# Two transformer layers on one core: 288 pairs of row maxima beside the projections in place of 223, and twelve pairs per eight key tiles in attention

## The chip, the core and the metric

The kernel runs on one core of a Trainium2 chip. The metric is device time in microseconds for one execution of the whole program, median of the runs. Inputs and outputs are float32 and lie in HBM.

## The reference

Two layers, each an attention block and a block with a squared ReLU, each with a layer norm ahead and a residual sum. The same weights serve both layers. There are 2048 rows of width 640, 32 heads of width 20, and a hidden width of 1536.

```python
def _A_ref(x, wqkv, wo):
    qkv = (x @ wqkv).reshape(B, S, 3, H, Dh)         # -> q, k, v per head
    scores = einsum("bhqd,bhkd->bhqk", q, k) * Dh ** -0.5
    o = einsum("bhqk,bhkd->bhqd", softmax(scores), v)
    return o.reshape(B, S, D) @ wo
def _B_ref(x, w1, b1, w2, b2):
    r = maximum(x @ w1 + b1, 0)
    return (r * r) @ w2 + b2

x = x + _A_ref(_layernorm(x), wqkv, wo)
x = x + _B_ref(_layernorm(x), w1, b1, w2, b2)
# ... and both once more
```

The softmax needs the largest score of each row before it exponentiates. What the change moves is the search for these maxima.

## The kernel before, in words

**Stages.** Each layer runs the projections (`qkv`), attention (`attention`), the output projection (`add_heads`) and the squared-ReLU block (`mlp`), one after the other. Between them q, k and v pass through HBM (`d_qk`, `d_v`).

**Blocks and tiles.** Heads are taken in eight groups of four (g = 0 to 7), queries in four blocks of 512 (qb). A block of attention is t = 4 g + qb, 32 in all. Keys are loaded in four quarters of 512 (c), one tile per group and quarter (`load_k`, L396), queries in one tile per block (`load_q`, L409), each with six DMAs on SP's queue. The key tiles are kept in three sets: group g takes the set g % 3, so the fourth group (g = 3) takes the memory of the first. Within attention a block goes over 16 key tiles of 128 keys (kt); this makes 512 key tiles in a layer.

**Two passes over the scores.** The kernel makes the scores twice. In the first pass the queries are rows, and VectorE takes each row's maximum over a quarter of the keys (the *maxima*). A unit of this work is a *pair*: two heads at once, 128 queries against one quarter of the keys, two matmuls (`by_queries`, L433). There are 8 pairs per block and quarter, 1024 in a layer. In the second pass, in attention, the keys are rows: one matmul per head and key tile (`score`, L499), with the negative maxima in two further rows of the query tile, then ScalarE's exponential (L506), then the products with v (`pv`, L511). The maxima of a block must all be there before its second pass: `mrows_max` (L462) joins the quarters, `mrows` (L474) transposes them on TensorE, and eight DMAs write them into the query tile.

**Where the maxima are made.** Some of the pairs run beside the projections: there TensorE makes two matmuls into two neighbouring banks, and VectorE reduces both with one instruction of 128x1024 (`smax_two`, L454). The others run inside attention, one bank and one instruction of 128x512 for each head (`smax`, L445), in a ring of three banks.

**Order beside the projections.** `qkv` emits 40 units of 15 matmuls (`proj_unit`, L304) and 16 units of 30 smaller ones for v (`v_unit`, L332). After each matmul it calls `between`, which adds 1 (0.65 in `v_unit`) to a counter; at 11 it emits three pairs in a burst (`some`). What it takes them from is `groups`, a list of (g, qb, c), each of eight pairs; when it begins one, it loads the tiles of that and of the next (`tiles`). The list is filled from `EARLY` as blocks of rows are projected: the first group of heads, and at the end of the first 16 units all sixteen entries of the second. At the end of the projections what is left of the list is dropped, and its pairs go to attention. Here this comes to 223 pairs per layer.

**Order in attention.** The engines' order is written out by strings in `ORDERS`: a and b are scores of even and odd heads, m and n the same for maxima, V the products of one key tile. One string covers eight key tiles (a *group of eight tiles* in what follows) with a given number of pairs, 12 to 16. `pairs()` chooses the string: it computes how many pairs per eight tiles are needed so that every block's maxima are made in time, and takes at least twelve. Over the 61 strings that have maxima left to make, before the change this is thirteen nearly everywhere and fourteen in five; the last strings make none. The string of twelve is there, but not used:

```python
13: "baanmbVmbanambbnbmVanbmnaVnaabnmbVanbmaanVnmbbanaVmnbmabVabbmmnaVm",
12: "naambbmVanmbambVbmannabVnabnmabVabnmbanVbbmnanaVbmmbaanVbmbmnaaV",
```

`op` emits one letter. For m and n it takes the next pair from `todo`; it emits nothing while that pair's keys or queries have not been asked for (`if (t // NQB, c) not in k_t or t not in q_t: return`). Keys are asked for in `begin(i)`, at the first score of key tile i: with block 4 (the first of g = 1, key tiles 64 to 79) come the four quarters of g = 3, at key tiles 65, 69, 73 and 77.

**Queues.** All these loads and stores are issued by SP in the order of the program. At the end of a block `finish` (L519) copies the sums out of the bank on ScalarE and stores four rows of them (`d_s`); these stores wait for the last product of the block, and what SP issues next stands behind them.

Of the kernel before, what the change touches and what calls it, by code (L numbers as in the profile page):

```python
# [25 lines left out]
NQB = S // QB  # L26
# [12 lines left out]
def tile_layers(  # L39
# [343 lines left out]
    k_t, q_t, v_t, mx_t, kept = {}, {}, {}, {}, {}  # L383
# [210 lines left out]
        [(0, qb, c) for qb in range(NQB) for c in range(NQB) if max(qb, c) == tb]  # L594
        for tb in range(NQB)
    ]
    EARLY[-1] += [(1, qb, c) for qb in range(NQB) for c in range(NQB)]

    FIRST = 4
    UNITS = [(tb, pos) for tb in range(NQB) for pos in range(FIRST)]
    UNITS += [(tb, pos) for pos in range(FIRST, 10) for tb in range(NQB)]

    def qkv(first, x_src, rest):
# [4 lines left out]
        state = {"pace": 0, "n": 0}  # L610
# [13 lines left out]
            else:  # L624
                at(early, n, lambda pos=pos: w_qk.need(pos * 10, pos * 10 + 9))
        for k in range(KD if first else w_v.n):
            n = len(UNITS) - 7 + k
            if first:
                at(early, n - 2, lambda k=k: raws.append(raw_rows(wqkv[:, 2 * D :], k)))
                at(late, n, lambda k=k: w_v.put(  # L630
                    raws.pop(0), k * 4, k * 4 + 2, 2, nc.scalar.copy, pool_lo
                ))
            else:
                at(early, n, lambda k=k: w_v.load(k))
# [18 lines left out]
        def end_group(x):  # L653
            g, qb, c = x
            t = g * NQB + qb
            left[t] -= 1
            if left[t]:
                return
            if t < 1:
                mrows_max(t)  # L660
                work.append(lambda: mrows(ps_q, t))
            elif t > 2:
                del q_t[t]
# [20 lines left out]

        def between(cost):
            state["pace"] += cost
            if state["pace"] >= 11:
                state["pace"] -= 11
                some()
            state["n"] += 1  # L690
            if state["n"] % 4 == 0:
                next(rest, None)

        for n, (tb, pos) in enumerate(UNITS):
            while tb not in xt_:
                next(rest)
            run(early, n)
            later(proj_unit(pos, tb, lambda: between(1)))
            run(late, n)
            if pos == FIRST - 2:  # L700
                tiles(EARLY[tb][0])
            if pos == FIRST - 1:
                groups.extend(EARLY[tb])
            if first:
                w_qk.save_full(1)
                w_v.save_full(1)
            if pos >= FIRST and tb == NQB - 1 or n == 4 * FIRST - 1:
                w_qk.past(pos * 10 + 9, w_qk.got)
# [370 lines left out]
```

## Time and profile before

| What | Value |
|---|---|
| Median of three runs | 3805.72 us (3802.45 to 3811.96) |
| The profiled execution | 3801.84 us, span 3799.8 us |
| TensorE's granted clock | 0.997 |
| Busy over the span | PE 3754.3, VectorE 2923.8, ScalarE 2399.9, GpSimd 813.0 us |
| Layer 1: first product of attention to the end of the last | 337.38 to 1487.87 us |
| Layer 2: the same | 2227.55 to 3376.36 us |
| Maxima beside the projections (L454), both layers | 446 instructions, 1220 ns each |
| Maxima in attention (L445), both layers | 3204 instructions, 685 ns each |

In the profile PE is TensorE's matmuls and PEld its weight loads; DVE is VectorE, ACT ScalarE, POOL GpSimd, and SPq SP's queue of DMA issues. Lines of a timeline begin with the start and the length in us and end in brackets with the idle time of the engine before and what ended it. Instructions of a kind that follow each other closely are one line, with their count behind the x. Matmuls are pipelined and their ends are modelled, so where TensorE's pace matters, the distance between starts is read and not the busy time. L511 has eight records per key tile.

### The profile page before, as it was taken

The page shows a single profiled execution, that of the slowest core. Times are in us where ns is not written, and L with a number is a line of the kernel's source. Part 1 is how long each engine was busy: PE and PEld are TensorE (multiplying, and loading weights), DVE is VectorE, ACT ScalarE, POOL GpSimd, SP SyncE. Part 2 cuts the span into 40 slices and gives each one's busy share as a digit, 9 for nine tenths or more (in the row PEclk, how much of TensorE's full clock was granted, in tenths as well). Part 3 has the DMA queues.
Part 4 walks back from the last instruction along what each step waited for, and adds up shares of the span by engine and source line. Part 5 has one row for each costly group of instructions (what it writes and reads, how often), then busy time and mean ns, then how long its engine had stood idle before and what let it go on. Part 6 is the DMA issues. An engine that isn't in the chain of part 4 may idle for free.

```text
span 3799.8 us, 62979 instructions
## 1 busy us (share of the span) xinstructions
PE 3754.3 (99%) x23636; PEld 2142.9 (56%) x23636; DVE 2923.8 (77%) x4436; ACT 2399.9 (63%) x4663; POOL 813.0 (21%) x889
## 2 busy tenths in 40 slices
PE   7999999999999999999999999999999999999999
PEld 5676444443443435988876754444444444369998
DVE  7999999999999992444469989999999999924443
ACT  2115999999999996122211159999999999951221
POOL 5430343221121111111143201211211111101110
PEclk9999999999999999999999999999999999999999
DMA  6553454322121135611244422222222211355111
GB/s 191 176 189 110 132 142 149 107 71 73 49 70 42 31 96 176 239 42 42 93 142 157 161 89 59 65 74 53 65 81 53 59 40 42 101 191 209 42 42 42
DMA packets 228073, 378.72 MB, mean 100 GB/s; under 512 B 47740, under 2 KB 96636, under 8 KB 227768
## 3 DMA queue, kind: packets, MB, share of 16 engines
q1 hardware_dynamic: 227224, 372.98, 31.1%
q8 instruction: 187, 3.06, 0.3%
q10 hardware_dynamic: 544, 1.71, 0.2%
q14 instruction: 118, 0.97, 0.1%
HBM read 243.00 MB, written 130.52 MB: 98 GB/s over the span
## 4 chain that ended last, share of the span: by engine, by line
PE 94%; DVE 3%; DMA 1%; ACT 1%; SPq 0%; issue 0%; POOL 0%; ACTq 0%; DVEq 0%; POOLq 0%
PE banks L511 26%; PE banks L293 20%; PE banks L499 18%; PE banks L433 18%; PE banks L304 6%; PE banks L332 4%; DVE mx L445 1%; DVE mx L454 1%; SPq L75 0%; PE banks L909 0%; PE banks L474 0%; ACT e L506 0%; DMA k<-d_qk 0%; DVE bst L252 0%; DVE h L265 0%
## 5 line engine op out<-in xcount | busy, mean ns | idle before, releaser
L506 ACT ACTIVATE e<-banks 128x512 f32<-128x512 f32 x4096 | 2113.8, 619 | 159.4 <-PE banks L499 104.7
L445 DVE TENSOR_REDUCE mx<-banks 128x1 f32<-128x512 f32 x3204 | 2002.5, 685 | 209.4 <-PE banks L433 147.5
L433 PE MATMUL banks<-k,q 60*128 60x512 f32 x4096 | 1197.5, 442 | 8.7 <-DMA q<-d_qk 4.1
L499 PE MATMUL banks<-q,k 62*128 62x512 f32 x4096 | 1174.9, 430 | 4.5 <-ACT e L506 1.7
L511 PE MATMUL banks<-e,vg 128*32 128x512 f32 x8192 | 1092.8, 605 | 0.0
L433 PEld LDWEIGHTS banks<-k,q 60*128 60x128 f32 x4096 | 580.7, 184 | 626.9 <-DVE mx L445 495.3
L499 PEld LDWEIGHTS banks<-q,k 62*128 62x128 f32 x4096 | 613.6, 185 | 438.6 <-ACT e L506 399.9
L454 DVE TENSOR_REDUCE mx<-banks 128x2 f32<-128x1024 f32 x446 | 518.8, 1220 | 49.6 <-PE banks L433 37.0
L555 POOL TENSOR_TENSOR few<-few,minus_t 128x16 f32<-128x16 f32 x62 | 179.8, 2901 | 991.1 <-DMA few<-d_s 975.3
L511 PEld LDWEIGHTS banks<-e,vg 128*32 128x32 f32 x8192 | 161.5, 108 | 346.0 <-issue 322.8
L293 PE MATMUL banks<-w,h 128*128 128x320 f32 x2304 | 352.8, 312 | 2.9 <-DVE h L265 2.7
L293 PEld LDWEIGHTS banks<-w,h 128*128 128x128 f32 x2304 | 340.9, 189 | 12.5 <-DVE h L265 6.8
L293 PE MATMUL banks<-xnT,w 128*128 128x512 f32 x1440 | 330.3, 390 | 0.0
L304 PE MATMUL banks<-xnT,wqk 128*128 128x512 f32 x1200 | 311.9, 407 | 0.0
L932 ACT ACTIVATE r<-banks,b_t 128x512 f32<-128x512 f32 x96 | 66.2, 690 | 375.2 <-PE banks L293 375.2
L293 PEld LDWEIGHTS banks<-xnT,w 128*128 128x128 f32 x1440 | 269.4, 188 | 55.3
L270 ACT COPY r<-banks 128x512 f32<-128x512 f32 x92 | 53.7, 588 | 334.9 <-PE banks L304 292.5
L304 PEld LDWEIGHTS banks<-xnT,wqk 128*128 128x128 f32 x1200 | 220.8, 192 | 68.9 <-issue 23.8
L952 DVE TENSOR_TENSOR x<-banks,x 128x320 f32<-128x320 f32 x128 | 62.8, 491 | 200.9 <-PE banks L293 194.9
L566 POOL TENSOR_TENSOR o<-o 128x512 f32<-128x512 f32 x62 | 79.5, 1282 | 560.0 <-PE banks L433 177.4
L933 DVE TENSOR_TENSOR r<-r 128x512 f32<-128x512 f32 x96 | 79.4, 827 | 132.6 <-ACT r L932 132.2
L887 DVE TENSOR_TENSOR x<-banks,x 128x320 f32<-128x320 f32 x64 | 31.0, 484 | 171.0 <-PE banks L293 77.7
(63 smaller groups left out, 1704.1 us busy)
## 6 DMA issues: line engine op xcount, KB each, us to landing
q<-d_qk SPq DMA_DIRECT2D x636, 80.0 KB
d_qk<-ev SPq DMA_DIRECT2D x80, 512.0 KB
k<-d_qk SPq DMA_DIRECT2D x384, 80.0 KB
x<-d_x SPq DMA_DIRECT2D x96, 320.0 KB
d_o<-ot SPq DMA_DIRECT2D x248, 80.0 KB
ot<-d_o SPq DMA_DIRECT2D x38, 512.0 KB
d_v<-v SPq DMA_DIRECT2D x32, 512.0 KB
vg<-d_v SPq DMA_DIRECT2D x32, 512.0 KB
```

The source lines that it names most:

```text
L293: nc.tensor.matmul(dst, a, b, start=(n == 0), stop=(n == last))
L304: nc.tensor.matmul(dst, w_qk.piece(pos * 10 + hw * KD + k), xt_[tb][k][:, hx, :], start=(n == 0), stop=(n == 3 * KD - 1),)
L332: nc.tensor.matmul(dst[:, :HALF], xt_[tb][k][:, hx, i * P : (i + 1) * P], w_v.piece(k * 4 + hw * 2 + hf), start=(j == 0), stop=(j == 3 * K ...
L433: nc.tensor.matmul(dst, q_t[t][b : b + 60, p, sub * P : (sub + 1) * P], k_t[t // NQB, c][b : b + 60, p, :], start=True, stop=True,)
L445: nc.vector.tensor_reduce(maxima(t)[:, 2 * p + par, sub, c : c + 1], dst, axis=AX.X, op=ALU.max)
L454: nc.vector.tensor_reduce(maxima(t)[:, 2 * p : 2 * p + 2, sub, c], dst, axis=AX.X, op=ALU.max)
L499: nc.tensor.matmul(dst, k_t[t // NQB, kt // 4][b : b + 62, p, (kt % 4) * P : (kt % 4 + 1) * P], q_t[t][b : b + 62, p, :], start=True, stop ...
L506: nc.scalar.activation(es[p][:, par, :], dst, AF.Exp, scale=SCALE)
L511: nc.tensor.matmul(acc[32 * h : 32 * h + 32, :], v_t[t // NQB, kt // 8][:, kt % 8, 32 * h : 32 * h + 32], es[p][:, par, :], start=(kt == 0 ...
L555: nc.gpsimd.tensor_tensor(few, few, minus_t, op=ALU.pow)
L566: nc.gpsimd.tensor_mul(o[:, 0, :], o[:, 0, :], o[:, 1, :])
L933: nc.vector.tensor_mul(r, r, r)
```

## The change

Five edits, all in what sets the order; no instruction is new.

- `EARLY` has the sixteen entries of the second and of the third group of heads; the first of them, (1, 0, 0), is taken out of the list.
- That one is put on the list at unit 5, while the second block of rows is being projected.
- `between` emits a burst of three pairs for every 8.7 counted, in place of 11.
- In the first layer the weights for v are prepared two units later.
- A query tile of the second group or later is given back when the next entry on the list is of another block.

```diff
-    EARLY[-1] += [(1, qb, c) for qb in range(NQB) for c in range(NQB)]
+    EARLY[-1] += [(g, qb, c) for g in (1, 2) for qb in range(NQB) for c in range(NQB)][1:]
...
-            n = len(UNITS) - 7 + k
+            n = len(UNITS) - (5 if first else 7) + k
...
             left[t] -= 1
             if left[t]:
+                if t >= NQB and groups and groups[0][:2] != (g, qb):
+                    del q_t[t]
                 return
...
             state["pace"] += cost
-            if state["pace"] >= 11:
-                state["pace"] -= 11
+            if state["pace"] >= 8.7:
+                state["pace"] -= 8.7
                 some()
...
             if pos == FIRST - 1:
                 groups.extend(EARLY[tb])
+            if n == FIRST + 1:
+                groups.append((1, 0, 0))
```

With this 288 pairs stand beside the projections of each layer: the first and the second group of heads, and the first block of the third. 736 are left for attention, which is twelve for each of 61 strings.

Three places show the order before and after, all of layer 1. First TensorE in the middle of the projections, from one burst of three pairs (L433, `k` and `q` are the tiles read) to the next; L304 are the projections' matmuls, `xnT` the normalised rows and `wqk` the weights. Before:

```order
L433 MATMUL banks<-k_797,q_964 128x512 x6
L304 MATMUL banks<-xnT_502,wqk_869 128x512 x3
L304 MATMUL banks<-xnT_521,wqk_869 128x512 x2
L304 MATMUL banks<-xnT_521,wqk_1030 128x512
L304 MATMUL banks<-xnT_534,wqk_869 128x512 x2
L304 MATMUL banks<-xnT_534,wqk_1030 128x512
L304 MATMUL banks<-xnT_547,wqk_869 128x512 x2
L433 MATMUL banks<-k_797,q_964 128x512 x6
```

After:

```order
L433 MATMUL banks<-k_1009,q_356 128x512 x6
L304 MATMUL banks<-xnT_215,wqk_1099 128x512
L304 MATMUL banks<-xnT_317,wqk_928 128x512 x3
L304 MATMUL banks<-xnT_328,wqk_928 128x512 x2
L304 MATMUL banks<-xnT_328,wqk_1099 128x512
L304 MATMUL banks<-xnT_339,wqk_928 128x512
L433 MATMUL banks<-k_1009,q_356 128x512 x6
```

Between two bursts stood eleven matmuls, and now stand eight (elsewhere nine).

Second TensorE in attention, from the products of one key tile (L511, `e` the exponentials, `vg` the values) to those of the next; L499 are scores, L433 maxima. Before, in the string of thirteen, its longest gap:

```order
L511 MATMUL banks<-e_5223,vg_4026 32x512 x2
L511 MATMUL banks<-e_5218,vg_4026 32x512 x2
L433 MATMUL banks<-k_3097,q_4315 128x512
L499 MATMUL banks<-q_4423,k_1710 128x512 x2
L433 MATMUL banks<-k_3097,q_4315 128x512
L499 MATMUL banks<-q_4423,k_1710 128x512
L433 MATMUL banks<-k_3097,q_4315 128x512
L499 MATMUL banks<-q_4423,k_1710 128x512 x2
L433 MATMUL banks<-k_3097,q_4315 128x512
L499 MATMUL banks<-q_4423,k_1710 128x512
L433 MATMUL banks<-k_3097,q_4315 128x512
L511 MATMUL banks<-e_5259,vg_4026 32x512 x2
```

After, in the string of twelve, one of its eight gaps:

```order
L511 MATMUL banks<-e_5779,vg_4225 32x512 x2
L511 MATMUL banks<-e_5774,vg_4225 32x512 x2
L499 MATMUL banks<-q_5010,k_530 128x512
L433 MATMUL banks<-k_607,q_5163 128x512 x2
L499 MATMUL banks<-q_5010,k_530 128x512 x2
L433 MATMUL banks<-k_607,q_5163 128x512
L499 MATMUL banks<-q_5010,k_530 128x512
L511 MATMUL banks<-e_5813,vg_4225 32x512 x2
L511 MATMUL banks<-e_5810,vg_4225 32x512 x2
```

The gaps of a string of thirteen have six, seven or eleven matmuls; those of the string of twelve all have seven.

Third the place where the fourth group of heads is first needed, with buffer numbers: `k50` is the key tile of the first quarter. SP's queue at the end of block 3 before (`d_s` the stores of its sums, `q429` the queries of block 6, `raw` weights):

```order
L75 DMA d_s_103<-o427_4414 1x512 x4
L75 DMA q429_4423<-d_qk_99 20x2x512 x6
L75 DMA k50_347<-d_qk_99 20x2x512 x6
L75 DMA raw435_4475<-in_B_w1_dram 128x5x128
L75 DMA few428_4416<-d_s_103 128x16
L75 DMA k84_572<-d_qk_99 20x2x512 x6
```

After:

```order
L75 DMA d_s_103<-o429_4583 1x512 x4
L75 DMA q431_4590<-d_qk_99 20x2x512 x6
L75 DMA k50_347<-d_qk_99 20x2x512 x6
L75 DMA q434_4609<-d_qk_99 20x2x512 x6
L75 DMA raw439_4654<-in_B_w1_dram 128x5x128
L75 DMA few430_4585<-d_s_103 128x16
L75 DMA k87_607<-d_qk_99 20x2x512 x6
```

The load of `k50` stands where it stood; a load of queries has come between it and that of the second quarter. What moved is its reader on TensorE. Before, the first maxima on it follow the products of key tile 97:

```order
L511 MATMUL banks_74<-e521_5254,vg383_4026 32x512 x2
L499 MATMUL banks_74<-q429_4423,k191_1710 128x512
L433 MATMUL banks_74<-k273_3097,q416_4315 128x512
L499 MATMUL banks_74<-q429_4423,k200_1807 128x512
L433 MATMUL banks_74<-k50_347,q473_4825 128x512 x2
L499 MATMUL banks_74<-q429_4423,k191_1710 128x512
L511 MATMUL banks_74<-e524_5281,vg383_4026 32x512 x2
```

After, they follow the products of key tile 63, the last of block 3:

```order
L511 MATMUL banks_74<-e426_4550,vg241_3016 32x512 x2
L511 MATMUL banks_74<-e425_4543,vg241_3016 32x512 x2
L499 MATMUL banks_74<-q337_3804,k76_530 128x512 x2
L433 MATMUL banks_74<-k50_347,q367_4059 128x512
L499 MATMUL banks_74<-q337_3804,k76_530 128x512 x2
L433 MATMUL banks_74<-k50_347,q367_4059 128x512
L511 MATMUL banks_74<-e428_4568,vg387_4225 32x512 x2
L511 MATMUL banks_74<-e427_4563,vg387_4225 32x512 x2
```

The first use of these keys is 34 key tiles earlier. The three other quarters are asked for at key tiles 69, 73 and 77, and their first maxima follow the products of key tiles 68, 73 and 79.

## Prediction

> **What bounds the kernel now.** I read the page first, then the busy times by stage, then the timelines of three places. By stage (columns: stretch, its length, then the busy time of PE, PEld, DVE, ACT and POOL with instruction counts, PE's clock, DMA) the stretches are the projections and the attention of layer 1, and the projections of layer 2:
>
> ```profile
> 0.00:334.00 334.00, 311.70 (x1607) 229.85 (x1607) 295.69 (x310) 59.83 (x113) 131.62 (x175) 0.98 0.52 174
> 334.00:1487.00 1153.00, 1150.59 (x7776) 459.52 (x7777) 1004.52 (x1634) 1071.84 (x2111) 281.60 (x290) 1.00 0.32 92
> 1960.00:2223.00 263.00, 261.46 (x1386) 192.86 (x1387) 248.95 (x215) 32.32 (x64) 68.59 (x83) 0.99 0.45 152
> ```
>
> In the projections VectorE is busy for 249 of 263 us: the maxima there run close to VectorE's pace. In attention no engine but PE is full: VectorE has 1004.5 of 1153, ScalarE 1071.8. A busy PE proves little, so I looked at what spaces its steps. In PE's timeline of attention (layer 1) each L511 row starts the products of one key tile; between two such rows lie its four scores and some maxima's matmuls.
>
> ```profile
> 624.73 1.06 PE L511 MATMUL banks<-e,vg 128*32 128x512 f32 x8
> ...
> 626.86 1.07 PE L511 MATMUL banks<-e,vg 128*32 128x512 f32 x8
> ...
> 630.17 1.07 PE L511 MATMUL banks<-e,vg 128*32 128x512 f32 x8
> ```
>
> ```profile
> 644.97 1.06 PE L511 MATMUL banks<-e,vg 128*32 128x512 f32 x8
> ...
> 662.82 1.06 PE L511 MATMUL banks<-e,vg 128*32 128x512 f32 x8
> ...
> 699.38 1.06 PE L511 MATMUL banks<-e,vg 128*32 128x512 f32 x8
> ```
>
> From 624.73 to 626.86 seven matmuls lie between the products, and the tile takes 2.13 us. The string of thirteen pairs has one gap of eleven: the next tile takes 3.31. A group of eight tiles takes 17.85 (644.97 to 662.82), the one before it, with a transposition of maxima in it, 18.11 (626.86 to 644.97). So attention goes at the pace at which TensorE gets through its order, with ScalarE not far below.
>
> **Part 1: 65 more pairs beside the projections of each layer.** VectorE's timeline in layer 2: start, hole, a long run, end of the stretch. Then TensorE's weight loads around one burst of three pairs:
>
> ```profile
> 1942.98 9.59 DVE L454 TENSOR_REDUCE mx<-banks 128x2 f32<-128x1024 f32 x8 [1.49 <-PE banks L433]
> 1961.43 3.49 DVE L454 TENSOR_REDUCE mx<-banks 128x2 f32<-128x1024 f32 x3 [8.87 <-PE banks L433]
> ...
> 2130.71 28.55 DVE L454 TENSOR_REDUCE mx<-banks 128x2 f32<-128x1024 f32 x24 [0.20 <-PE banks L433]
> ...
> 2206.39 17.90 DVE L454 TENSOR_REDUCE mx<-banks 128x2 f32<-128x1024 f32 x15 [0.25 <-PE banks L433]
> ```
>
> ```profile
> 2079.35 0.30 PEld L433 LDWEIGHTS banks<-k,q 60*128 60x128 f32 x4 [0.35 <-issue]
> 2079.81 0.19 PEld L433 LDWEIGHTS banks<-k,q 60*128 60x128 f32 x2 [0.16 <-DVE mx L454]
> 2080.25 2.38 PEld L304 LDWEIGHTS banks<-xnT,wqk 128*128 128x128 f32 x11 [0.25 <-issue]
> 2082.98 0.30 PEld L433 LDWEIGHTS banks<-k,q 60*128 60x128 f32 x4 [0.35 <-issue]
> ```
>
> A burst comes every 3.63 us (2079.35 to 2082.98), in which TensorE waits 0.16 for a bank: TensorE, at 3.47, and VectorE are nearly level. Reductions overlap; one lasts 1.22 (the page's 518.8 busy is not their sum for that reason). Inside a burst one starts every 1.135 us ((3.49 - 1.22) / 2), over many bursts every 1.19 ((28.55 - 1.22) / 23). With 8.7 units between bursts in place of 11, TensorE has 2.3 matmuls fewer, each about 0.23 (eleven and two switches take 2.73 from 2080.25), so a burst is 2.94 for it. VectorE alone then sets the pace, at 3 x 1.135 = 3.40. TensorE's own added work, 130 matmuls and 22 more bursts, is hidden behind that: 96 x 2.94 = 282 against VectorE's 327. Without that cover only what stands above 327 would count.
>
> By the Trainium skill, TensorEngine Tiling (Array Packing), Key Properties, a change of tiling mode drains the TensorEngine, which speaks against more and shorter bursts. The trace agrees in so far as the weight loads idle 0.35 and 0.25 at the burst's edges; by that rule 22 more bursts cost 13 us of a TensorE that has 45 to spare, so the sum is the same.
>
> In layer 2 the stretch from 1942.98 to 2224.29 is 281.3: 223 x 1.194 = 266 at the present spacing, 15 other waits. After: 288 x 1.135 = 327 and about 5, since the early eight pairs of the second group of heads (9.1 us) go into the hole of 8.87. That is 332, or +50. Layer 1 has the same bursts and as much idle time to fill, so I take **+100** in all. Bounds: +45 a layer if all the other waits go, +67 if the spacing stays at 1.194 (288 x 0.059 = 17 more).
>
> The Trainium skill, VectorE: DVE Perf Modes, in the section on the TRN2 errata, gives a VectorE instruction out of PSUM 120 cycles plus one per element at 0.96 GHz: an estimate of 1.19 us for 1024 elements, by which this part is +67 a layer. The row of three in 3.49 lies below it, so the sum stays with the row.
>
> **Part 2: twelve pairs per eight key tiles in attention.** The string of twelve has seven matmuls in every gap. First and last product of the 61 groups of layer 1 that hold maxima, and ScalarE in the last groups, which hold none:
>
> ```profile
> 337.38 1.73 PE L511 MATMUL banks<-e,vg 128*32 128x512 f32 x8
> ...
> 1438.98 1.07 PE L511 MATMUL banks<-e,vg 128*32 128x512 f32 x8
> ```
>
> ```profile
> 1455.64 0.61 ACT L524 COPY o<-banks 128x512 f32<-128x512 f32 x1
> 1456.11 30.65 ACT L506 ACTIVATE e<-banks 128x512 f32<-128x512 f32 x60
> ```
>
> The 61 groups take 1101.6, or 18.06 each (five of them are strings of fourteen). From below: 8 x 2.13 = 17.04, and 0.26 (18.11 - 17.85) in every second group for the transposition: 17.17. ScalarE needs 32 x 30.65 / 60 = 16.3 and a copy of 0.6 every second group, 16.6, so it has half a microsecond of room and will at times hold a bank too long. From above: the groups from 662.82 to 699.38 hold 54 maxima and take 36.56, two usual ones hold 52 and take 35.96; at 0.3 a maximum, two fewer in a group of 17.98 give 17.4. I take 17.3: 1055 in place of 1101.6, **-46 a layer, -92 in all**. Bounds: 17.1 gives -58 a layer, 17.7 (half of 0.3) gives -22.
>
> **Part 3: keys that come late.** From block 9 on, twelve pairs per eight tiles reach the fourth group of heads at key tile 64, where its keys are only being loaded. Between the products of tiles 63 and 64 TensorE now has maxima on those keys, and their load stands on SP behind the stores of block 3's sums, which need tile 63's product, and a query load. Today's times, layer 1 and layer 2 (L511 is tile 63's product; 2384.01 is tile 69's), and a load early in layer 1 with the matmul that waited for it:
>
> ```profile
> 480.93 1.07 PE L511 MATMUL banks<-e,vg 128*32 128x512 f32 x8
> ```
>
> ```profile
> 482.95 1.48 SPq L75 DMA_DIRECT2D d_s<-o  x4
> 485.14 3.70 SPq L75 DMA_DIRECT2D q<-d_qk  x6
> 488.88 2.23 SPq L75 DMA_DIRECT2D k<-d_qk  x6
> ```
>
> ```profile
> 2370.02 1.06 PE L511 MATMUL banks<-e,vg 128*32 128x512 f32 x8
> ...
> 2384.01 1.06 PE L511 MATMUL banks<-e,vg 128*32 128x512 f32 x8
> ```
>
> ```profile
> 2375.43 2.24 SPq L75 DMA_DIRECT2D k<-d_qk  x6
> ...
> 2393.31 2.64 SPq L75 DMA_DIRECT2D k<-d_qk  x6
> ```
>
> ```profile
> 57.35 2.42 SPq L75 DMA_DIRECT2D k<-d_qk  x6
> ```
>
> ```profile
> 62.99 0.93 PE L433 MATMUL banks<-k,q 60*128 60x512 f32 x5 [1.07 <-DMA k<-d_qk]
> ```
>
> There TensorE went on 3.2 us after the last issue (59.77 to 62.99). So the keys are there at 491.1 + 3.2 = 494.3 and at 2377.7 + 3.2 = 2380.9, and are wanted when the product (1.07) and a pair or two are through, about 1.5 after its start: 482.4 and 2371.5. TensorE stands for 11.9 and 9.4, the next scores are queued behind, and ScalarE and VectorE run dry. The second quarter's keys are issued while TensorE stands, and are in time. The third quarter's come behind the stores of a block's maxima: issued by 2395.95, there at 2399.2, 15.1 after tile 69's product; wanted after four more tiles (8.5, a transposition 0.26) and 1.5, at 10.3. That is 4.8 more; I take it for both layers. **+31** (21.3 + 9.6). Bounds: +16 (half, if SP gets there sooner) and +46.
>
> **The rest.** Giving a tile of queries back issues nothing. The early group's fourteen DMAs take SP 0.4 each (2.42 / 6), 5.6 us, ahead of ev's stores and x's rows, which the units need a unit or more later; without that cover 5.6 a layer. The values' weights, made two units later in layer 1, are for ScalarE and GpSimd, busy 60 and 132 of 334; without that cover TensorE waits there once, for less than a burst.
>
> **The sum.** 100 - 92 + 31 = +39, and one for the rest: +40. The profiled execution took 3801.84, so 3842; the median of the runs shown is 3.9 above that execution, so 3846.
>
> **The rivals.** *Attention falls to ScalarE's own pace (faster).* If the groups lose TensorE's gaps and run at 16.6, a layer gains 89: 100 - 178 + 31 = -47, or 3759. It decides from 16.98 a group on (131 / 122 under 18.06). For it: the last groups do so. Against: every gap of seven above takes 2.13. 0.08. *No late keys.* If SP is further ahead than today, part 3 is gone: +8, or 3814, within 0.3% (11 us, about what a measurement of this kernel can tell from no change). For it: most loads are early. Against: the stores ahead of this one wait for tile 63 itself. 0.14. *VectorE keeps 1.19.* +134 in part 1, or 3880. For it: the long rows of today. Against: their gaps are ended by PE, which gets time to spare. 0.13. *ScalarE holds the groups at 17.7.* -44 in part 2, or 3894. For it: the small room. 0.10. That the change doesn't do what it says is out: in the order of each layer 576 of these matmuls stand in the projections.
>
> **How the numbers follow.** The forecast has 0.55. Slower by over 0.3%: 0.55 + 0.13 + 0.10 = 0.78; within: 0.14; faster: 0.08. The range, 3808 to 3884, holds the forecast with bounds that partly cancel (-38 and +38 around it: part 2's are the widest, 24 and 48), the second rival and the third, and leaves out 3759 and 3894, 0.18 together.
>
> **What would show it.** In the projections the reductions follow each other with few gaps ended by PE, 288 in some 330 us, and the matmuls of L433 wait for DVE mx L454. In attention the usual group takes 17.2 to 17.4, and TensorE stops twice a layer for a DMA of k, once for about 10 us. I am wrong if the projections grow by under 40 a layer, if groups are below 17, or if no matmul waits long for k.

## The result and the profile after

The changed kernel takes **3870.2 us** (median of 4 runs, 3868.2 to 3875.5), the kernel before 3805.6 (3802.5 to 3812.0): ratio **1.017, 95% interval 1.0152 to 1.0187**, so 65 us slower. The profiled execution of the changed kernel took 3875.5, with a span of 3873.7; its span is 73.9 above that of the profile before, and it is these 73.9 that the stages below account for. (The executions profiled lie 5.3 above and 3.8 below their medians, which is why the medians differ by 65.)

The busy times by stage, of the changed kernel: projections and attention of layer 1, then of layer 2 (length, then PE, PEld, DVE, ACT, POOL with instruction counts, PE's clock, DMA):

```profile
0.00:401.80 401.80, 362.93 (x1738) 243.89 (x1738) 364.78 (x375) 60.46 (x115) 131.08 (x175) 0.97 0.46 152
404.00:1535.00 1131.00, 1109.96 (x7643) 444.33 (x7642) 929.48 (x1502) 1068.84 (x2107) 281.54 (x290) 0.99 0.32 92
1985.00:2330.50 345.50, 329.68 (x1614) 218.03 (x1613) 327.72 (x290) 37.37 (x73) 81.61 (x97) 0.99 0.41 134
2332.50:3450.50 1118.00, 1106.22 (x7641) 443.69 (x7641) 929.24 (x1502) 1068.22 (x2107) 210.32 (x186) 0.99 0.25 67
```

The first product of attention comes at 404.45 in layer 1 (before: 337.38) and the last group that holds maxima ends at 1486.01. In layer 2 it is 2332.94 and 3401.76, in PE's timeline:

```profile
404.45 0.64 PE L511 MATMUL banks<-e,vg 128*32 128x512 f32 x4
...
1486.01 1.07 PE L511 MATMUL banks<-e,vg 128*32 128x512 f32 x8
...
2332.94 0.64 PE L511 MATMUL banks<-e,vg 128*32 128x512 f32 x4
...
3401.76 0.64 PE L511 MATMUL banks<-e,vg 128*32 128x512 f32 x4
```

| stretch | before | after | difference |
|---|---|---|---|
| start to the first product of attention, layer 1 | 337.4 | 404.5 | +67.1 |
| 61 groups of attention, layer 1 | 1101.6 | 1081.6 | -20.0 |
| projections of layer 2 (end of attention 1 to first product of attention 2) | 739.7 | 798.4 | +58.7 |
| 61 groups of attention, layer 2 | 1100.3 | 1068.8 | -31.5 |
| what is left: the groups after these in both layers, and the end | | | -0.4 |

(The third row holds the output projection and the block behind it as well; up to the first reduction of layer 2 these take 455.1 before and 455.9 after.) So the projections cost 126 and attention gave 52 back. VectorE's timeline in layer 2, which answers to the one shown of before:

```profile
1990.42 9.15 DVE L454 TENSOR_REDUCE mx<-banks 128x2 f32<-128x1024 f32 x8 [1.60 <-PE banks L433]
2009.01 3.49 DVE L454 TENSOR_REDUCE mx<-banks 128x2 f32<-128x1024 f32 x3 [9.44 <-PE banks L433]
2014.22 5.75 DVE L454 TENSOR_REDUCE mx<-banks 128x2 f32<-128x1024 f32 x5 [1.73 <-PE banks L433]
2020.13 81.70 DVE L454 TENSOR_REDUCE mx<-banks 128x2 f32<-128x1024 f32 x72 [0.15 <-PE banks L433]
...
2105.94 224.36 DVE L454 TENSOR_REDUCE mx<-banks 128x2 f32<-128x1024 f32 x198 [0.64 <-PE banks L433]
```

(A "hole" is a long idle time of VectorE, a "burst" three pairs.) From 2105.94 on, 198 reductions follow each other closely, one every (224.36 - 1.23) / 197 = 1.133 us. The hole at the start is still there, 9.44 long. TensorE, which had waited 0.16 us a burst, now waits for VectorE in each (PE's weight loads, one burst to the next, 3.39 us):

```profile
2153.69 0.19 PEld L433 LDWEIGHTS banks<-k,q 60*128 60x128 f32 x2 [0.40 <-DVE mx L454]
2154.11 1.70 PEld L304 LDWEIGHTS banks<-xnT,wqk 128*128 128x128 f32 x8 [0.24 <-issue]
2156.18 0.30 PEld L433 LDWEIGHTS banks<-k,q 60*128 60x128 f32 x4 [0.36 <-DVE mx L454]
2157.08 0.18 PEld L433 LDWEIGHTS banks<-k,q 60*128 60x128 f32 x2 [0.60 <-DVE mx L454]
```

In attention a usual pair of groups, the first with a transposition, takes 17.40 and 17.02 (group starts in layer 2):

```profile
2515.55 1.06 PE L511 MATMUL banks<-e,vg 128*32 128x512 f32 x8
...
2532.95 1.06 PE L511 MATMUL banks<-e,vg 128*32 128x512 f32 x8
...
2549.97 1.06 PE L511 MATMUL banks<-e,vg 128*32 128x512 f32 x8
```

TensorE stops twice a layer for keys, and what SP does ahead of the first stop of layer 2 is the stores of sums, a query load, then the keys:

```profile
552.26 0.76 PE L433 MATMUL banks<-k,q 60*128 60x512 f32 x1 [10.45 <-DMA k<-d_qk]
580.45 0.80 PE L433 MATMUL banks<-k,q 60*128 60x512 f32 x2 [5.05 <-DMA k<-d_qk]
...
2479.29 0.76 PE L433 MATMUL banks<-k,q 60*128 60x512 f32 x1 [8.85 <-DMA k<-d_qk]
...
2505.51 0.80 PE L433 MATMUL banks<-k,q 60*128 60x512 f32 x2 [2.44 <-DMA k<-d_qk]
```

```profile
2470.69 1.10 SPq L75 DMA_DIRECT2D d_s<-o  x4
2471.89 2.18 SPq L75 DMA_DIRECT2D q<-d_qk  x6
2474.12 2.73 SPq L75 DMA_DIRECT2D k<-d_qk  x6
```

And layer 1 has a stop that the prediction did not have. Near 777 us ScalarE waits 3.8 us for GpSimd to finish with a slot (a piece of SBUF that several kinds of tiles take in turn), GpSimd had waited 15 for a load, and TensorE waits for ScalarE (timelines of POOL, ACT and PE):

```profile
773.80 1.26 POOL L566 TENSOR_TENSOR o<-o 128x512 f32<-128x512 f32 x1 [15.02 <-DMA o<-d_r]
...
777.11 3.54 ACT L506 ACTIVATE e<-banks 128x512 f32<-128x512 f32 x7 [3.77 <-POOL ot L278]
...
777.76 1.77 PE L499 MATMUL banks<-q,k 62*128 62x512 f32 x3 [3.64 <-ACT e L506]
```

The two groups there take 18.37 and 25.46 in place of 17.0 and 17.4, which is 9.4 us. Just before, at 769.35 and 772.74, two of ScalarE's exponentials had waited 1.39 and 1.33 us for a store of weights (`d_w`).

### The profile page after: what moved, and what is told of

It reads as the page before. It is cut to its first block, busy times and chain, and to the rows that moved or that the text cites. A ratio compares the mean times of both kernels' runs of the same rounds, so it can differ in the third digit from the quotient of the medians.

```text
span 3873.7 us, 62898 instructions
## 1 busy us (share of the span) xinstructions
PE 3770.4 (97%) x23636; PEld 2137.6 (55%) x23636; DVE 2911.5 (75%) x4306; ACT 2397.1 (62%) x4663; POOL 812.2 (21%) x889
## 4 chain that ended last, share of the span: by engine, by line
PE 77%; DVE 17%; DMA 2%; SPq 1%; ACT 1%; POOL 1%; issue 0%; ACTq 0%; POOLq 0%; DVEq 0%
PE banks L511 26%; PE banks L293 19%; PE banks L499 19%; DVE mx L454 15%; PE banks L433 11%; SPq L75 1%; PE banks L304 1%; DMA k<-d_qk 1%; DVE bst L252 0%; PE banks L913 0%; PE banks L474 0%; PE banks L362 0%; DMA q<-d_qk 0%; DVE h L265 0%; DVE x L260 0%
## 5 line engine op out<-in xcount | busy, mean ns | idle before, releaser
L445 DVE TENSOR_REDUCE mx<-banks 128x1 f32<-128x512 f32 x2944 | 1852.2, 685 | 304.6 <-PE banks L433 185.4
L433 PE MATMUL banks<-k,q 60*128 60x512 f32 x4096 | 1240.5, 443 | 58.3 <-DMA k<-d_qk 29.8
L499 PE MATMUL banks<-q,k 62*128 62x512 f32 x4096 | 1167.9, 436 | 7.7 <-ACT e L506 5.5
L511 PE MATMUL banks<-e,vg 128*32 128x512 f32 x8192 | 1097.8, 607 | 0.0
L499 PEld LDWEIGHTS banks<-q,k 62*128 62x128 f32 x4096 | 609.0, 186 | 672.2 <-ACT e L506 618.9
L433 PEld LDWEIGHTS banks<-k,q 60*128 60x128 f32 x4096 | 564.6, 186 | 446.7 <-DVE mx L445 212.3
L454 DVE TENSOR_REDUCE mx<-banks 128x2 f32<-128x1024 f32 x576 | 654.4, 1217 | 39.7 <-PE banks L433 39.6
L511 PEld LDWEIGHTS banks<-e,vg 128*32 128x32 f32 x8192 | 161.9, 108 | 358.2 <-issue 334.4
L304 PE MATMUL banks<-xnT,wqk 128*128 128x512 f32 x1200 | 324.2, 414 | 0.0
L936 ACT ACTIVATE r<-banks,b_t 128x512 f32<-128x512 f32 x96 | 66.1, 688 | 377.5 <-PE banks L293 375.0
L304 PEld LDWEIGHTS banks<-xnT,wqk 128*128 128x128 f32 x1200 | 221.4, 194 | 74.0 <-issue 31.2
L956 DVE TENSOR_TENSOR x<-banks,x 128x320 f32<-128x320 f32 x128 | 62.8, 491 | 200.8 <-PE banks L293 191.8
L341 ACT COPY v<-banks 128x320 f32<-128x320 f32 x64 | 27.3, 426 | 216.7 <-PE banks L332 203.9
```

Of the source, the lines that this page charges most:

```text
L304: nc.tensor.matmul(dst, w_qk.piece(pos * 10 + hw * KD + k), xt_[tb][k][:, hx, :], start=(n == 0), stop=(n == 3 * KD - 1),)
L433: nc.tensor.matmul(dst, q_t[t][b : b + 60, p, sub * P : (sub + 1) * P], k_t[t // NQB, c][b : b + 60, p, :], start=True, stop=True,)
L445: nc.vector.tensor_reduce(maxima(t)[:, 2 * p + par, sub, c : c + 1], dst, axis=AX.X, op=ALU.max)
L454: nc.vector.tensor_reduce(maxima(t)[:, 2 * p : 2 * p + 2, sub, c], dst, axis=AX.X, op=ALU.max)
L499: nc.tensor.matmul(dst, k_t[t // NQB, kt // 4][b : b + 62, p, (kt % 4) * P : (kt % 4 + 1) * P], q_t[t][b : b + 62, p, :], start=True, stop ...
L511: nc.tensor.matmul(acc[32 * h : 32 * h + 32, :], v_t[t // NQB, kt // 8][:, kt % 8, 32 * h : 32 * h + 32], es[p][:, par, :], start=(kt == 0 ...
```

## The experiments

The theory: VectorE at 1.133 us a reduction sets the pace of the projections, so 65 more pairs cost there nearly in full, more than twelve pairs a group give back in attention, and late keys take a part of that too. Against it stand: TensorE sets the pace, with its changes of tiling mode (from matmuls of 128 rows to such of 60 and back); the keys' stops are only moved time; attention gains nothing by twelve.

### Does VectorE set the pace of the projections?

`e4_half_maxima`, in `smax_two`:

```diff
-            maxima(t)[:, 2 * p : 2 * p + 2, sub, c], dst, axis=AX.X, op=ALU.max
+            maxima(t)[:, 2 * p : 2 * p + 2, sub, c], dst[:, :, : QB // 2], axis=AX.X, op=ALU.max
```

> The changed kernel, whose reductions beside the projections read only half of each bank (128x2x256 in place of 128x2x512), so that the maxima over the other half of the keys are left out there; TensorE's order is the same. Theory (VectorE alone sets the pace of the projections): a burst falls from 3.40 us to TensorE's 2.94, so 96 x 0.46 = 44 a layer, 3782 us, 3772 to 3800. Rival (TensorE's changes of tiling mode and its waits, not the reductions, set the pace): 3860 to 3872.

Measured 3804.7 us (0.9996 of before, 0.9986 to 1.0005), 65 under the changed kernel, level with the kernel before, and 5 above the theory's range. The projections are 32.5 us shorter in layer 1 and 32.0 in layer 2, attention 4.8 in layer 1 and not at all in layer 2. VectorE's rows and PE's weight loads in layer 2:

```profile
1984.62 1.89 DVE L454 TENSOR_REDUCE mx<-banks 128x2 f32<-128x512 f32 x3 [1.25 <-PE banks L433]
1987.77 1.89 DVE L454 TENSOR_REDUCE mx<-banks 128x2 f32<-128x512 f32 x3 [1.27 <-PE banks L433]
```

```profile
2067.38 0.53 PEld L433 LDWEIGHTS banks<-k,q 60*128 60x128 f32 x6 [0.35 <-issue]
2068.27 1.91 PEld L304 LDWEIGHTS banks<-xnT,wqk 128*128 128x128 f32 x9 [0.37 <-issue]
2070.54 0.53 PEld L433 LDWEIGHTS banks<-k,q 60*128 60x128 f32 x6 [0.35 <-issue]
2071.43 1.68 PEld L304 LDWEIGHTS banks<-xnT,wqk 128*128 128x128 f32 x8 [0.37 <-ACT r L270]
2073.46 0.53 PEld L433 LDWEIGHTS banks<-k,q 60*128 60x128 f32 x6 [0.35 <-issue]
```

VectorE now idles 1.25 a burst, and its pace was the bound: shown, since TensorE's order is the same and only the reductions are shorter. The gain is 32 a layer and not 44 because TensorE's own burst is 3.16 with nine matmuls between (2067.38 to 2070.54) and 2.92 with eight, on the mean of 8.7 about 3.1, not 2.94: its weight loads idle 0.35 and 0.37 at the edges. By the Trainium skill, TensorEngine Tiling (Array Packing), Key Properties, a change of tiling mode drains the TensorEngine. The trace has idle time at these places, but no run shows that the drain is its cause, and in the changed kernel it stays hidden behind VectorE.

### The early group

`e2_no_early` puts the eight pairs back into the list; `f4_early_ready` asks for them a unit sooner:

```diff
-    EARLY[-1] += [(g, qb, c) for g in (1, 2) for qb in range(NQB) for c in range(NQB)][1:]
+    EARLY[-1] += [(g, qb, c) for g in (1, 2) for qb in range(NQB) for c in range(NQB)]
...
-            if n == FIRST + 1:
-                groups.append((1, 0, 0))
```

```diff
-            if n == FIRST + 1:
+            if n == FIRST:
                 groups.append((1, 0, 0))
+                tiles((1, 0, 0))
```

> The changed kernel without its early eight pairs of the second group of heads (they go back to their old place in the list; 280 pairs a layer beside the projections in place of 288). Theory (the early group came no sooner than the group that it pushed back, so the hole of VectorE stayed at 9.4 us and TensorE waited some 6 us for its queries): projections shorter by 8 x 1.135 = 9 a layer, attention longer by 16 maxima at about 0.3 = 5 a layer, 3858 us, 3850 to 3866. Rival, the reading in the prediction (the eight pairs run in the hole at no cost): projections as long as before this edit, attention 5 a layer longer, 3880.

> The changed kernel, whose early group of the second group of heads is asked for one unit sooner, ahead of the store of the fifth unit. Theory (the early pairs miss the hole only because their loads stand behind that store): the hole of 9.4 us in layer 2 falls below 4 and the wait of 5.4 for q goes, some 6 to 9 a layer, 3855 us, 3850 to 3862. Rival (the loads stand behind the stores of the third and fourth unit as well, which they need): under 3 a layer, 3865 to 3872.

`f4_early_ready` took 3857.3 (1.0136 of before, 1.0121 to 1.0151), a time that the theory had, but not all of it for the theory's reason. Its start of layer 2 has two holes of 2.6 and 3.3 in place of one of 9.4, the wait of 5.4 for q is gone, and the projections are 4.7 shorter (5.9 in layer 1), a little under the 6 to 9 expected. Another 7 of the 18.5 between the two profiles lie in the attention of layer 1, whose stops came out shorter; the edit does not touch them, and the execution of the changed kernel that was profiled is its slowest. VectorE's timeline:

```profile
1986.38 1.23 DVE L454 TENSOR_REDUCE mx<-banks 128x2 f32<-128x1024 f32 x1 [0.82 <-PE banks L433]
1990.23 8.01 DVE L454 TENSOR_REDUCE mx<-banks 128x2 f32<-128x1024 f32 x7 [2.62 <-PE banks L433]
2001.54 81.61 DVE L454 TENSOR_REDUCE mx<-banks 128x2 f32<-128x1024 f32 x72 [3.30 <-PE banks L433]
```

In the changed kernel the early group's loads stand on SP behind a store that SP waits for from 1985.96 to 1998.87, and TensorE reaches their matmuls before they are there:

```profile
1985.96 12.91 SPq L75 DMA_DIRECT2D d_qk<-ev  x3
...
1999.69 2.42 SPq L75 DMA_DIRECT2D k<-d_qk  x6
2002.15 2.30 SPq L75 DMA_DIRECT2D q<-d_qk  x6
```

```profile
2006.83 0.76 PE L433 MATMUL banks<-k,q 60*128 60x512 f32 x1 [5.35 <-DMA q<-d_qk]
```

`e2_no_early` took 3833.1 (1.0066, 1.0049 to 1.0083), 37 less than the changed kernel and less than either side expected. Its hole is 10.7, no shorter than with the early group, and its projections are 9.7 and 10.0 shorter, which is the eight pairs. But attention fell too, by 13.6 and 5.9, where it has 16 maxima more. With 16 more to do first, the maxima reach the late keys later (TensorE stops after the products of key tile 67, not 63), the stops shrink to one a layer of 3.5 and 1.4 us, and the one for slots near 777 is gone. So most of what was unexpected here belongs to the keys, and `f2_keys_no_early` (next) bears it out.

### The late keys

`e1_keys_in_time` puts the maxima off; `f1_keys_sooner` asks for the keys sooner, at tile i for what was asked for at tile i + 12 (`now` is the key tile that was begun last, `asked` the one at which keys were asked for):

```diff
                 if (t // NQB, c) not in k_t or t not in q_t:
                     return
+                if now[0] < asked[t // NQB, c] + 8:
+                    return
```

```diff
-            if u % 4 == 1 and qb == 0:
-                k_t.pop((g - 1, u // 4), None)
+            for j in {i + 12, i} if i < NKT else {i + 12}:
+                f, v = j // NKT // NQB, j % NKT
+                if v % 4 == 1 and j // NKT % NQB == 0 and f < NG:
+                    k_t.pop((f - 1, v // 4), None)
...
```

> The changed kernel, but a maximum is not taken until eight key tiles after its keys were asked for. Theory (the two stops a layer for a DMA of k cost the excess of their groups, about 20 us in layer 1 and 16 in layer 2, and the maxima put off are taken later for nothing): 3834 us, 3828 to 3842, no matmul of L435 waiting over 1 us for k in attention. Rival (the stop is only moved: the maxima put off come due in strings of 14 to 16, or TensorE waits for the next thing): 3862 to 3872. The stop of about 10 us in layer 1 near 777 us, where ScalarE waits for a slot, is not touched by this on either reading; if it goes as well, the time is about 3824.

> The changed kernel, but each quarter of the keys of two groups ahead is asked for twelve key tiles sooner, as soon as the quarter whose slot it takes has had its last score. Nothing is put off. Theory (holding the maxima back gave 12 of 20 and 13 of 16 us a layer back as strings of fourteen, so the stops themselves do cost about 20 and 16): 3834 us, 3826 to 3840, all groups of layer 2 at 17.0 to 17.4 but for the strings of fourteen of today; 8 us less if the stop near 777 us in layer 1 goes too. Rival (the stops hide a wait that attention has to make anyway): 3862 to 3872.

> Keys asked for twelve tiles sooner and no early group: 280 pairs a layer beside the projections. Theory (without the early group the late keys still cost 8 and 2 us): 3833 less 10, 3823 us, 3817 to 3830. Rival (the gain of leaving the early group out was that of the late keys, which are gone here already, so that 8 pairs fewer beside the projections and 16 maxima more in attention cancel): as f1_keys_sooner, 3834.

`e1_keys_in_time` took 3856.8 (1.0132, 1.0117 to 1.0147), between the two: no matmul of attention waited over 1 us for k, the stop near 777 went too, and still only 13 of 36 to 46 came back. Two neighbouring groups of it, by PE's timeline (here L513), take 16.85 and 18.76:

```profile
2471.35 1.06 PE L513 MATMUL banks<-e,vg 128*32 128x512 f32 x8
...
2488.20 1.07 PE L513 MATMUL banks<-e,vg 128*32 128x512 f32 x8
...
2506.96 0.64 PE L513 MATMUL banks<-e,vg 128*32 128x512 f32 x4
```

That is 35.61 for 50 maxima, where two strings of twelve take 34.42 for 48. The maxima have due times, and those put off came back as strings of thirteen: by the order of TensorE's matmuls each layer has 14 of them in place of 2 (and one string with next to no maxima), and 12 x 1.2 is 14 of the 17.8 that the stops of layer 2 were worth. "Taken later for nothing" was wrong. The expectations of `f1_keys_sooner` and `f3_pace_10` speak of strings of fourteen here; this run has none.

`f1_keys_sooner` took 3836.6 (1.0083, 1.0068 to 1.0098), within 3 of the theory. In layer 2 the 61 groups take 1051.0 (2313.93 to 3364.90), 17.8 less than in the changed kernel and 49.3 less than before. Layer 1 lost its stops for keys and got two for slots (groups of 26.1 and 22.9), so it gained 15.4:

```profile
581.00 3.54 ACT L506 ACTIVATE e<-banks 128x512 f32<-128x512 f32 x7 [4.30 <-POOL ot L278]
...
724.10 3.53 ACT L506 ACTIVATE e<-banks 128x512 f32<-128x512 f32 x7 [2.88 <-POOL ot L278]
```

`f2_keys_no_early` took 3837.8 (1.0085, 1.007 to 1.01), the same as `f1_keys_sooner`: with the keys in time, eight pairs fewer beside the projections (-7.6 and -9.0) and 16 maxima more in attention (+5.2 and +10.3) cancel. The rival was right. So the 37 us of `e2_no_early` are those of the stops that went: its groups with stops hold 8.2 and 2.0 us over their usual time, where the changed kernel's 61 groups have 30.6 (9.4 of it for slots) and 17.8 over the 1051.0 of `f1_keys_sooner`, 38 more.

### Attention alone

`e5_attention_alone` is the kernel before, with the third group in the list and, at the end of `qkv`:

```diff
+        skip = 65
+        while skip:
...
+            (g, qb, c), p, sub = w
+            nc.gpsimd.memset(maxima(g * NQB + qb)[:, 2 * p : 2 * p + 2, sub, c], 0.0)
+            done.add((g * NQB + qb, p, sub, c))
+            skip -= 1
...
```

> The kernel before (223 pairs a layer beside the projections, no early group), but the next 65 pairs of the changed kernel's list are set to zero by GpSimd and not computed, so that attention has the 1464 x 2 maxima of the changed kernel while the projections are as before. Theory (the attention of the changed kernel differs from before by the -20.0 and -31.5 us that the trace gives for the 61 groups): 3754 us, 3744 to 3764, with two stops a layer for k and groups alternating between 17.0 and 17.4. The prediction's own terms (-92 + 31) give 3745. The rest of the change's cost, 3870 less this, is then that of the 65 pairs beside the projections: 116 on the theory, 125 on the prediction's terms with the measured total. Rival (twelve in place of thirteen gains nothing by itself, attention is held elsewhere): 3795 to 3810.

Measured 3773.0 (0.9913, 0.9898 to 0.9928): between the theory and the rival, but for a reason of its own. Attention begins with maxima of the third group, whose queries and keys are here only asked for then:

```profile
347.97 0.76 PE L433 MATMUL banks<-k,q 60*128 60x512 f32 x1 [10.38 <-DMA q<-d_qk]
...
367.36 0.76 PE L433 MATMUL banks<-k,q 60*128 60x512 f32 x1 [5.71 <-DMA k<-d_qk]
```

```profile
2224.60 0.79 PE L433 MATMUL banks<-k,q 60*128 60x512 f32 x1 [9.02 <-DMA q<-d_qk]
...
2243.16 0.76 PE L433 MATMUL banks<-k,q 60*128 60x512 f32 x1 [4.57 <-DMA k<-d_qk]
```

From the last reduction of the projections to the end of attention's first group it takes 20.5 and 18.1 longer than the changed kernel, which no other kernel does. Without them it would be 3734; that is worked out, not measured. It is 20 under the theory's 3754: this kernel has no stop for slots (9.4), and the groups at its stops for keys are 3.0 and 4.5 shorter than in the changed kernel, which is 17 of it. Its attention makes 1472 maxima a layer, as the changed kernel's does, and its usual groups of 24 alternate between 17.0 and 17.4 from the second on, so the rival falls: twelve gains by itself.

### The stop near 777 us

`g1_saves_later` is `f1_keys_sooner` with

```diff
-            if first and t < 16 and u == 8:
+            if first and t < 16 and u == 13:
```

> As f1_keys_sooner (3836.6), and in layer 1 the finished weights are stored at key tile 13 of a block in place of tile 8, so that SP's stores of weights (three of 0.6 to 0.85 us each) and their traffic no longer stand ahead of the load of a block's inverted sums, on which GpSimd waits before it gives back the slots that ScalarE's next exponentials take. Theory (the stops of layer 1 that remain, groups of 26.1 and 22.9 us in place of 17.4 and 17.0, come from that): 14 less, 3823 us, 3819 to 3828, no exponential of layer 1 waiting over 1 us for GpSimd. Rival (slots are short there whatever SP does, because tiles of queries and keys are held longer): 3833 to 3840.

Measured 3843.8 (1.0102, 1.0084 to 1.012): the rival, 4 above its range. The stops stay; only what they wait for has changed:

```profile
585.25 4.03 ACT L506 ACTIVATE e<-banks 128x512 f32<-128x512 f32 x8 [3.67 <-DMA d_w<-w]
...
733.17 3.04 ACT L506 ACTIVATE e<-banks 128x512 f32<-128x512 f32 x6 [5.24 <-DMA d_w<-w]
```

The exponential's slot is one that something else still holds, there GpSimd's product, here a store of weights. Layer 2, where no weights are made, has no such stop of over 1 us in any kernel. That slots run short while weights are made and the maxima run further ahead fits most of this: with 240 pairs beside the projections (`g5_mended_10`, below) there is none. It does not fit all: `e5_attention_alone` makes as many maxima in attention as the changed kernel and has none either. No kernel here had more slots, so the cause stays open.

### The pace between, and versions that could beat both

`f3_pace_10` is `f2_keys_no_early` with 8.7 replaced by 10 in `between`; `g5_mended_10` is the changed kernel with the edits of `f1_keys_sooner`, `g1_saves_later` and `f4_early_ready` and 10.5; `g3_half_mended` has these three edits and that of `e4_half_maxima` at 8.7; `g2_before_ready` is the kernel before with

```diff
-    EARLY[-1] += [(1, qb, c) for qb in range(NQB) for c in range(NQB)]
+    EARLY[-1] += [(1, qb, c) for qb in range(NQB) for c in range(NQB)][1:]
...
+            if n == FIRST:
+                groups.append((1, 0, 0))
+                tiles((1, 0, 0))
```

> As f2_keys_no_early with a burst every 10 units in place of 8.7: 244 pairs a layer beside the projections. Theory (VectorE sets the pace of the projections at 1.135 a pair down to about the 223 pairs of the kernel before; in attention a pair costs 0.78 as the thirteenth of a string of thirteen, up to 1.2 as the thirteenth and fourteenth of one of fourteen): 36 x 2 x (1.135 - 0.78) = 26 less than f2_keys_no_early, 3797, 3795 to 3825. Rival (TensorE sets the pace there, as the long rows of the kernel before with gaps ended by PE suggest): projections shorter by less than 20 a layer, and the time above 3830.

> The changed kernel with the three mends that leave nothing out (keys twelve tiles sooner, stores of weights at tile 13, the early group a unit sooner) and a burst every 10.5 units, 240 pairs a layer beside the projections. Theory (f3_pace_10 had 244 pairs, no early group and took 3828; eight pairs now go into holes, so 12 fewer lie on VectorE's path at about 1.0 each, attention has 8 maxima more at 0.3, and 2 us of the slot stop go): 3806 us, 3800 to 3812, level with the kernel before. Rival (the third group of heads beside the projections costs something of its own): 3815 or more.

> The kernel before with an early group alone: the eight pairs of (1,0,0), asked for at once after the fourth unit's store, in its hole; the rest of the list, the pace and attention's thirteen as before (230 pairs a layer, 14 maxima a layer fewer for attention). Theory (work put into a hole costs nothing beside the projections, and attention saves about 0.28 a maximum): 4 less a layer, 3797 us, 3793 to 3801. Rival (the loads only move the hole): 3803 to 3812.

> The changed kernel with keys twelve tiles sooner, stores of weights at tile 13, the early group asked for a unit sooner, and reductions beside the projections over half of each bank as in e4_half_maxima (the maxima over the other half are left out there). Theory (the parts add: -66 for the halves, -34 for the keys, -13 for the early group, -14 for the stores of weights): 3743 us, 3738 to 3765. Rival (with VectorE out of the way the early group's and the keys' gains are hidden by TensorE): 3770 to 3790.

| kernel | pairs a layer | projections 1, 2 | attention 1, 2 | time | ratio to before |
|---|---|---|---|---|---|
| before | 223 | 293.7, 281.3 | 1150.5, 1148.8 | 3804.3 | |
| `g2_before_ready` | 230 | 299.2, 283.9 | 1145.7, 1144.4 | 3800.3 | 0.9980 to 0.9999 |
| `g5_mended_10` | 240 | 312.9, 293.3 | 1141.5, 1142.8 | 3818.4 | 1.0022 to 1.0052 |
| `f3_pace_10` | 244 | 318.7, 294.7 | 1145.2, 1140.4 | 3828.2 | 1.0044 to 1.0077 |
| `f2_keys_no_early` | 280 | 349.7, 331.0 | 1119.9, 1109.8 | 3837.8 | 1.007 to 1.01 |
| the changed kernel | 288 | 359.8, 339.9 | 1130.1, 1117.3 | 3870.2 | 1.0152 to 1.0187 |
| `g3_half_mended` | 288, halves | 322.2, 303.1 | 1116.6, 1099.6 | 3770.5 | 0.9895 to 0.9927 |

(Projections from the first reduction to the end of the last, attention from its first product to the end of its last, in the profiled executions.)

**What a pair costs.** From 280 to 244 pairs, one pair is worth 0.86 to 1.01 us beside the projections and 0.70 to 0.85 in attention; `f3_pace_10` therefore gained only 10 where 26 were expected, and lies between what theory and rival had. Where the bound changes is read from the short waits of the reductions (what their spacing has over 1.133, waits of over 1.5 us apart): 2 to 8 us a layer with 280 or 288 pairs, about 11 with 244, 17 to 21 with 240 and fewer. TensorE's burst with eight matmuls between is 2.92 in `e4_half_maxima`, and one with ten, at 0.24 each, would be 3.40, which is VectorE's 3 x 1.133; that is worked out, not measured, and puts the crossing at the pace of 10, or 244 pairs.

`g5_mended_10` went the rival's way (3818), but its trace shows another reason than the third group: its short waits are 17 and 19 us a layer again, as in the kernel before (21 and 18), so TensorE had taken over as the bound and the twelve pairs fewer saved only 5.8 and 1.4 against `f3_pace_10`. `g2_before_ready` beats the kernel before by about 4 us, an interval that barely leaves 1 out, but, against its theory, the work put into the hole was not free. In the trace the projections grew by 5.5 and 2.6 and attention fell by 4.8 and 4.4, which leaves next to nothing, and the two profiles differ by 0.5 the other way. `g3_half_mended`, which leaves half of the maxima beside the projections out, is 34 us under the kernel before; its 3770.5 is at the rival's edge. It lacks 27 of the sum of its parts: the stores of weights, put at 14, gave nothing, and the attention of layer 1, which still has its stops for slots (groups of 24.2 and 24.8), is only 8.6 shorter than in `e4_half_maxima`, where the keys alone had given 15.4. The gains of the early group beside the projections (5 a layer) and of the keys in layer 2 (18) stayed, so the rival's reason was not it.

## Why the prediction was right, point by point

It forecast 3846 in a range of 3808 to 3884, slower; measured 3870. The mechanism was right: attention gains, the projections lose more. The size was less so: the change costs 65 by the medians and 74 between the two profiles, where the sum had 40. Part 1 was mis-sized most, parts 2 and 3 each missed by 8 and cancel, which is luck, and one term was not foreseen. The time by itself lies closer to the rival's 3880 ("VectorE keeps 1.19") than to 3846; what decides between them is the trace.

**What bounds the projections.** Right. VectorE sets the pace at 1.133 a reduction, as the row of three in 3.49 said, and the rival "VectorE keeps 1.19" fell: in a row of 198 the measured spacing is 1.133. With it fell, as a spacing, the estimate of 1.19 us from the Trainium skill, VectorE: DVE Perf Modes, the section on the TRN2 errata (120 cycles and one per element out of PSUM). TensorE's burst was put at 2.94 and is 3.1, which stayed hidden. (The spacing of 1.194 in its sum is 1.19 by the row that it shows, which moves the term by about 1 us.)

**Part 1, +100: +126 measured (67.1 and 58.7).** The step that failed is "the early eight pairs go into the hole of 8.87". That hole was taken to need work. But the loads that it waits for stand on SP behind a store that is not ready (15.55 us long in the kernel before), and the early group's loads came to stand behind the same store (12.91). Asked for sooner, as in `f4_early_ready`, they give 4.7 to 5.9 of 9.1 a layer back; what holds the rest is not shown. In layer 2, 65 pairs at 1.133 are 73.6; the short waits fell from 17.8 to 2.2, as said; the long ones, the hole among them, stayed (10.8 and 11.3); 73.6 - 15.6 + 0.5 = 58.5, and the trace has 58.6. In layer 1 the short waits gave 14.2 (20.7 to 6.5), but the long ones, among VectorE's layer-norm work and loads of queries, grew by 6.7 (20.2 to 26.9): 66.1, and the first reduction came 0.8 later. "Layer 1 has the same bursts and as much idle time to fill" was the same error once more.

**Part 2, -92: -100.** The groups take 17.0 and 17.4; without stops 61 of them take 1051.0 (`f1_keys_sooner`, layer 2), which is -50.6 and -49.3 against the 1101.6 and 1100.3 of before. Predicted were 1055 and -46. (By the order of the matmuls six of the 61 strings before have fourteen pairs and one has twelve, where the text has five and none. The number of pairs is the same, and no term moves.)

**Part 3, +31: +39.** The stops came where they were put, at 10.45 and 8.85 (predicted 11.9 and 9.4) and 5.05 and 2.44 (4.8). The price of a stop is more than its wait: taking them away gave 17.8 in layer 2, of which 11.3 were waits. The groups behind a stop run slowly as well (19.01 for the one after the first), and about 1.2 is one more string of thirteen. For layer 1, what its 61 groups have over 1051.0 is 30.6, less 9.4 for the slots: 21.2.

**Not foreseen: +9.4** for slots in layer 1. In the trace of before ScalarE waits in attention only once for GpSimd, 0.25 us, so nothing there pointed to it. Its cause stays open.

Together 125.8 - 99.9 + 39.0 + 9.4 = 74.3, against 73.9 between the two profiles. Without late keys and slots the change would still lose: 126 for 100. All three things that would have made it wrong stayed away: the projections grew by over 40 a layer, the usual groups stayed at 17.2 on the mean, and matmuls waited long for k.

## What to carry to other kernels

When work moves from one stage to another, price it in both stages by the engine that is the bound there, and look for the point where the bound changes: here VectorE had become the bound somewhere between 240 and 280 pairs, and from 244 on a pair cost 0.86 to 1.01 us to save 0.70 to 0.85. A hole helps only work whose data can be there when the hole begins, so follow its loads back through the queue before counting on it; even then the eight pairs here cost a part of their price. Work that runs further ahead meets its inputs' loads and the buffers' return earlier than anyone planned: of a gain of 100 in attention, 48 went back to late keys and slots.

## What the runs showed of the hardware that was not expected

- A reduction of 1024 columns out of PSUM starts every 1.133 us in a row of 198, one of 512 columns (0.69 long) every (1.89 - 0.69) / 2 = 0.60 in rows of three: 0.53 for 512 columns, so by these two sizes about 1.04 ns a column and 0.07 us fixed.
- At each edge of a burst TensorE's weight loads idle 0.35 and 0.37 us when nothing else holds them (`e4_half_maxima`), 0.7 a burst in all.
- Two stops of TensorE in attention, of 11.3 us together, cost 17.8 in layer 2, about 1.2 of it one more string of thirteen: ScalarE idles 8.47 and 3.03 us with them, and another 1.93 and 1.51 right behind each.
